# The last 256 rows of a two-layer attention and MLP kernel in two chunks of 128, and a longer planned latency for the DMAs that spread reciprocals

## The chip, the core and the metric

The kernel runs on one core of a Trainium2 chip. TensorE (PE) does the matrix products, ScalarE (ACT) the exponentials, VectorE (DVE) most other arithmetic, GpSimd (POOL) a few small sums and one kind of DMA; most DMAs are issued by SyncE (SP). The metric is the device time of one execution, in microseconds (us). Three executions of the kernel before took 1590.61, 1589.63 and 1586.18 us; their median is 1589.63 us. The trace is of one further execution, which took 1588.44 us.

## What is computed

Two equal layers are applied to x (2048 rows of 512, bf16). Each layer is attention with 32 heads of 16, and then a two-matrix MLP with 1792 hidden columns, each with a layer norm ahead of it and a residual sum behind it:

```
x = x + A(layernorm(x));  x = x + B(layernorm(x));  x = x + A(layernorm(x));  x = x + B(layernorm(x))
A(x): q, k, v = heads of x @ wqkv;  softmax(q k^T / 4) v, heads joined, @ wo
B(x): relu(x @ w1) @ w2
```

The 2048 x 2048 scores of 64 head-layers have to go through an exponential: 268 million of them. Output and inputs are bf16.

## The kernel before, in words

**Rows in chunks.** The rows are tiled by 128. A *chunk* (`chunks`, L460 to L464) is the set of query rows that goes through attention and MLP together: 512 rows (4 tiles) for all of layer one and for the first two chunks of layer two, and 256 rows (2 tiles) for layer two's last four, numbered 2 to 5; `LAST` is 5. For each chunk and each pair of heads (`T` from 0 to 3, and an even and an odd half `e`) there is a *segment* (L831): eight segments a chunk, each over 16 blocks of 128 keys and 4 row groups.

**The stream of exponentials.** The main loop (L1267) goes by slots. In each, PE makes scores into one of two groups of three PSUM banks (L1396), in units of 512 columns. In a chunk narrower than 512, a unit is several key blocks beside each other: two of 256. ACT turns three units (1536 columns) or two (1024) into exponentials with one instruction (L1405). Where it takes two, DVE makes the third by integer arithmetic (`dve_block` and `chain`, L1086 and L1126): `lin` (L1090), two `step` (L1131), two `cube` products (L1142, L1146), worked in pairs of units. PE then adds the products with the values into one PSUM bank, `ps_o` (L983). PE may repeat a round of scores in a slot where it would otherwise do too little (`times`, L1387).

**The end of a segment.** DVE copies `ps_o` to `u` (L897). Of each row's 512 or 256 sums the reciprocal is needed on all 16 lanes of a head: SP moves the sums to a small tile `c` (L902), DVE takes the reciprocal (L924), SP moves it back (L925), POOL spreads it with a further DMA to `r` (L927), and DVE multiplies (`ot`, L913). For the last segment of a chunk (`quick`, L921) the spreading is done on DVE instead (a shuffle, L937). The segment before the very last, and the last, take the reciprocal of all lanes on DVE without DMAs (`direct`, L941).

**The rest of a chunk** (`rest_of_chunk`, L795) are *groups* of PE work that fill the gaps between scores: the output projection `o_group` (L695), layer norm and transposes (`ln_rows`, `ln_groups`), the first MLP product `h_group` (L722), the second `z_group` (L762). An `h_group` fills a PSUM bank of 512 columns: one block of 128 hidden columns for a 512-row chunk, two for a 256-row chunk. The blocks of w1 (128 KB each) are loaded again for every chunk, through four buffers in turn (L710): a group's own loads are issued by SP as soon as its product is done, for the group two further on (L742 to L750).

**What sets the order.** The program writes all instructions in an order that a planner inside the kernel works out. It keeps a modelled clock of PE and of DVE (`now_pe`, `now_dve`), and the constants of L75 to L96 are its durations and latencies; `mark(key, lag=...)` records when a result is expected, and a DVE task is placed when its inputs are expected. Three of these constants are latencies of DMAs: `C_LAG` (`u` to `c`, 3.6 us), `R_LAG` (from the reciprocal through both moves to `r`, 10.5 us, L934) and `U_LAG` (from the reciprocal to `u` alone, 3.0 us). They delay nothing on the chip: every engine and queue works in the order written and waits for semaphores.

**The end of the program** (L1432 to L1528). After the last segment's value products the planner first writes whatever groups are left (`run_all`, L1436; their relu goes to ACT there, L734). Then a sequence by hand does the last chunk's rest: the output projection of its rows with the last heads from `direct` (L1461 to L1468), statistics and a reciprocal root in small DVE steps (L1469 to L1473), the second product for a row tile of the chunk before, left for this place (`half_part`, L1494), transposes, and a loop over 14 blocks of hidden columns (L1501) in which the product of a block's `h`, its relu (on DVE and ACT by turns) and the `z` product of the block before follow each other.

Of the kernel before, what the change touches and what calls it, by code (L numbers as in the profile page):

```python
# [12 lines left out]
BF16 = mybir.dt.bfloat16  # L13
# [12 lines left out]
def kernel(  # L26
# [11 lines left out]
    P = 128  # L38
# [3 lines left out]
    S, D = x_flat.shape  # L42
# [4 lines left out]
    NF = DFF // P  # L47
    NTT = S // P
    NKB = S // P
    NDC = D // P  # L50
    QS = 512
    NQS = S // QS
    TPC = QS // P
    NT = 8
# [22 lines left out]
    PE_TO_DVE, DVE_TO_PE, ACT_TO_PE, PE_TO_ACT = 220.0, 180.0, 240.0, 222.0  # L77
    DVE_TO_DVE, EVAC = 112.0, 612.0
    FLOOR = 0.56
    C_LAG, R_LAG, U_LAG = 3600.0, 10500.0, 3000.0  # L80
    VLAG = 1
    X_ISSUE, X_LAG = 1400.0, 7500.0
    RSTD_LAG = 4000.0
# [53 lines left out]
    xnT = [sb([P, NDC, QS], BF16, f"xnT{j}") for j in range(NQS)]  # L137
# [106 lines left out]
    busy = [0.0]  # L244
# [43 lines left out]
    def task(cost, fn, makes=(), deps=(), place=None):  # L288
        t = {"cost": cost, "fn": fn, "makes": makes, "deps": deps}
        dve_q.insert(len(dve_q) if place is None else place, t)  # L290
        maker.update({k: t for k in makes})
# [6 lines left out]
    def put_evac(cost, fn):  # L298
        evac.append((cost, now_pe[0] + PE_TO_DVE, fn))
# [159 lines left out]

    chunks = {(l, j): (j * TPC, TPC) for l in range(2) for j in range(NQS)}  # L460
    HALF = TPC // 2
    for n in range(4):
        chunks[1, 2 + n] = (2 * TPC + n * HALF, HALF)
    LAST = 5  # L464

    def columns(l, j):

# [118 lines left out]
    def ln_groups(tag, dst, at_column, n, war):  # L586
        groups = []
        for i in range(0, n, 2):
            hold = {}

            def piece(k):
                if not k % 2:
                    hold["b"] = bank()
                half = hold["b"].bitcast(BF16)[:, k % 2 * D : (k % 2 + 1) * D]
                ln_transpose(tag, k, half)
                if not k % 2:
                    return
                pt = hold["b"].bitcast(BF16).rearrange("p (i c f) -> p c i f", i=2, c=NDC)

                def fin():  # L600
                    a = at_column + (k - 1) * P
                    nc.vector.tensor_copy(
                        out=dst[:, :, a : a + 2 * P].rearrange("p c (i f) -> p c i f", i=2), in_=pt
                    )
                    for of in (k - 1, k):
                        mark(("xnT", tag, of))

                put_evac(609, fin)

            groups.append(  # L610
                group(
                    [(1.3, lambda k=k, piece=piece: piece(k)) for k in (i, i + 1)],
                    [("xT", tag, k) for k in (i, i + 1)] + [("xnT", tag, k) for k in (i, i + 1)],
                    [("xn", tag, k) for k in (i, i + 1)] + war,
                )
            )
        return groups
# [101 lines left out]

    w1_to_load = deque()  # L720

    def h_group(l, j, ft, war):  # L722
        n = (l * NQS + j) * NF + ft
        xj, a, w = columns(l, j)

        number = QS // w
        fts = range(ft, ft + number)
        made_here = [("h", l, j, f) for f in fts]

        def fin(b):  # L730
            out = htp[ft // 2][:, ft % 2 : ft % 2 + number, a : a + w]
            sums = b.rearrange("p (f q) -> p f q", f=number)
            if ending[0]:
                nc.scalar.activation(out=out, in_=sums, func=ACTF.Relu)  # L734
            else:
                nc.vector.tensor_scalar(  # L736
                    out=out, in0=sums, scalar1=0.0, scalar2=None, op0=ALU.max
                )
            for key in made_here:
                mark(key)  # L740

        def after():  # L742
            for f in range(number):
                load_w1(n + f + NW1)
            if w1_to_load:
                home, of = w1_to_load.popleft()
                nc.sync.dma_start(
                    out=home,
                    in_=B_w1[:, of * P : (of + 1) * P].rearrange("(c p) f -> p c f", p=P),
                )  # L750

        return mm_group(
            [
                (w1buf[(n + f) % NW1][:, c, :], xnT[xj][:, c, a : a + w])
                for f in range(number) for c in range(NDC)
            ],
            fin, made_here,
            each(w // P, "xnT", ("ln2", l, j)) + war + [("w1", n + f) for f in range(number)],
            after=after, wide_by=w, sums=number,
        )  # L760

    def z_group(l, j, i):  # L762
# [18 lines left out]
    def before(l, j):  # L781

        if (l, j) == (0, 0):
            return None
        if not j:
            return 0, NQS - 1
        rows = chunks[l, j][0] % TPC
        return max(
            (l, b) for b in range(j)
            if chunks[l, b][1] == TPC or chunks[l, b][0] % TPC == rows  # L790
        )

    w1_last = []
# [1 line left out]
    def rest_of_chunk(l, j):  # L795

        if (l, j) == (1, LAST - 2):
            for ft in range(NF):
                home = (
                    w1buf[((l * NQS + LAST) * NF + ft) % NW1] if ft < NW1  # L800
                    else (kt01 + kt2)[(ft - NW1) // 2][:, ft % 2, :].rearrange(
                        "p (c f) -> p c f", c=NDC
                    )
                )
                w1_last.append(home)
                if ft >= NW1:
                    w1_to_load.append((home, ft))
        b = before(l, j)
        xj, a, w = columns(l, j)
        n = w // P  # L810
        war_h = each(chunks[b][1], "z", *b) if b else []
        work[0:0] = [o_group(l, j, i) for i in range(n)] + ln_groups(
            ("ln2", l, j), xnT[xj], a, n, []
        )
        gs = [h_group(l, j, ft, war_h) for ft in range(0, NF, QS // w)]
        gs += [z_group(l, j, i) for i in range((l, j) == (1, LAST - 1), n)]
        if l == 0:
            if not by_dma(("ln1", 1, j)):
                gs += ln_groups(("ln1", 1, j), xnT[j], 0, TPC, [])
            gs.append(k_group(1, 0, j))  # L820
            gs += [v_group(1, kb) for kb in range(j * TPC, (j + 1) * TPC)]
            gs += [k_group(1, T, j) for T in range(1, 4)]
        return gs
# [38 lines left out]
    ended = {}  # L862
# [4 lines left out]
    def finish_segment(sg, last):  # L867
# [50 lines left out]
                mark(("ot", l, j, t, i))  # L918

        ended[l, j] = ended.get((l, j), 0) + 1  # L920
        quick = ended[l, j] == NT or sg["load"] is not None and sg["busy"]  # L921

        def recip():
            nc.vector.reciprocal(out=c, in_=c)  # L924
# [35 lines left out]
        if last:  # L960
            last_steps.append(direct)
        elif sg is segs[-2]:
            task(3100, direct_all, ots + [("m", n)], war + [("u", n)])
        else:
            task(165, recip, [("r", n)], [("c", n)], place=0)
            ready = ("r", n)
            if quick:
                task(200 + 1.05 * width, spread, [("spread", n)], [ready])
                ready = ("spread", n)
            task(105 + 1.1 * width, lambda: mul(0, width), ots + [("m", n)], [ready] + war)  # L970
# [588 lines left out]
```

The softmax here doesn't subtract the row's maximum and nothing guards it: scores larger than these inputs give would overflow.

## Time and profile before

| what | us |
|---|---|
| median of three executions | 1589.63 |
| the profiled execution | 1588.44 |
| its span, first to last instruction | 1586.6 |
| ACT busy in the span | 1545.3 |
| of it exponentials (L1405) | 1536.7 |
| DVE busy | 1506.7 |
| PE busy | 1430.4 |
| POOL busy | 101.3 |
| end of the last exponential to end of the span | 29 |

The instruction lines are the kernel's line numbers. Busy times are the union of an engine's instructions; matmuls overlap in the array, so a mean of one matmul is longer than the spacing of two. "Idle before" is time in which an engine had nothing running, with the instruction that ended it behind the arrow. A granted clock (PEclk) of 1.00 is full speed of TensorE and 0.50 half.

### The profile page before, as it was taken

The numbers are of one execution on the slowest core, as the hardware profiler recorded it, in microseconds if no ns is written. First come the engines' busy times: TensorE is split into PE (matmuls) and PEld (weight loads), VectorE is DVE, ScalarE is ACT, GpSimd is POOL, SyncE is SP. The second block draws the span as 40 slices with busy tenths as digits, with TensorE's granted clock in tenths as the row PEclk, the third lists the DMA queues.
The fourth block names the chain that finished last, engine by engine and source line by source line (L and its number), as shares of the span: only waits on it lengthen the run. The fifth ranks groups of instructions, "written<-read, shape, count | busy, mean of one in ns | idle before, by whom it ended". The sixth has DMA issues, their size and how long they took to land.

```text
span 1586.6 us, 45174 instructions
## 1 busy us (share of the span) xinstructions
PE 1430.4 (90%) x19752; PEld 536.9 (34%) x19752; DVE 1506.7 (95%) x2910; ACT 1545.3 (97%) x1383; POOL 101.3 (6%) x240
## 2 busy tenths in 40 slices
PE   8888889998899989999899998888999999999898
PEld 3222223222233322322223222223334444544454
DVE  7899999999999999999899998899999999999994
ACT  7999999999999999999999999999999999999994
POOL 2000001001010010100100001001001000010100
PEclk9999999999999999999999999999999999999998
DMA  6001101111012120120101000000210111313030
GB/s 193 15 2 26 18 9 22 39 25 25 6 19 45 23 29 7 25 48 13 26 2 28 21 2 1 2 4 9 54 25 16 40 33 27 74 26 80 13 62 15
DMA packets 128885, 45.57 MB, mean 29 GB/s; under 512 B 117840, under 2 KB 125776, under 8 KB 128688
## 3 DMA queue, kind: packets, MB, share of 16 engines
q1 hardware_dynamic: 114752, 29.36, 8.6%
q0 software_dynamic: 12592, 12.02, 4.3%
q8 instruction: 154, 2.52, 0.7%
q10 hardware_dynamic: 1344, 1.31, 0.2%
q14 instruction: 43, 0.35, 0.1%
HBM read 24.38 MB, written 2.10 MB: 17 GB/s over the span
## 4 chain that ended last, share of the span: by engine, by line
ACT 81%; PE 8%; DVE 7%; issue 2%; DMA 1%; ACTq 0%; DVEq 0%
ACT e L1405 81%; PE ps_s L1396 3%; PE ps_f L446 2%; DVE lin L1090 2%; PE ps_o L983 2%; DVE step L1131 1%; PE ps_s L1458 1%; DVE cube L1146 1%; DVE cube L1142 1%; DMA wqkv<-in_A_wqkv_dram 1%; DMA r<-u 0%; DVE ht L736 0%; DVE q L676 0%; DVE ot L913 0%; DVE stats L481 0%
## 5 line engine op out<-in xcount | busy, mean ns | idle before, releaser
L1405 ACT ACTIVATE e<-ps_s 128x1536 bf16<-128x1536 f32 (+1 forms) x1366 | 1536.7, 1362 | 8.5 <-PE ps_s L1396 8.1
L1396 PE MATMUL ps_s<-q,ktp 32*128 32x512 bf16 (+1 forms) x6136 | 608.1, 341 | 112.4 <-ACT e L1405 99.2
L983 PE MATMUL ps_o<-e,vaug 128*32 128x512 bf16 (+1 forms) x4236 | 500.8, 346 | 14.1 <-DVE u L897 8.3
L1090 DVE TENSOR_SCALAR lin<-ps_s 128x512 int16<-128x512 f32 x702 | 478.3, 685 | 24.5 <-PE ps_s L1396 18.1
L1396 PEld LDWEIGHTS <-ktp 32*128 32x128 bf16 x6136 | 200.3, 92 | 563.6 <-issue 418.9
L1131 DVE TENSOR_SCALAR step<-lin 128x1024 int16<-128x1024 int16 x702 | 275.3, 419 | 1.9 <-PE ps_o L983 0.9
L983 PEld LDWEIGHTS <-vaug 128*32 128x32 bf16 x6052 | 173.8, 95 | 300.9 <-issue 282.2
L1142 DVE TENSOR_TENSOR cube<-step 128x1024 f16<-128x1024 bf16 x351 | 238.4, 683 | 1.6 <-PE ps_o L983 0.2
L1146 DVE TENSOR_TENSOR cube<-cube,lin 128x1024 bf16<-128x1024 f16 x351 | 238.0, 679 | 0.0
L446 PE MATMUL ps_f<-w,ht 128*32 128x512 bf16 x1624 | 151.6, 381 | 1.8 <-DVE x L768 0.5
L446 PE MATMUL ps_f<-xnT,w 128*32 128x512 bf16 (+1 forms) x2016 | 146.3, 345 | 5.8 <-DVE ht L736 3.6
L983 PE MATMUL ps_o<-step,vaug 128*32 128x512 bf16 (+1 forms) x884 | 151.0, 340 | 0.0
L983 PE MATMUL ps_o<-cube,vthird 128*32 128x512 bf16 (+1 forms) x836 | 148.9, 339 | 0.0
L983 PE MATMUL ps_o<-lin,vaug 128*32 128x512 bf16 (+1 forms) x884 | 125.9, 339 | 4.6 <-DVE u L897 3.2
L927 POOL DMA_DIRECT2D r<-u x59 | 43.1, 731 | 1168.6 <-DVE lin L1090 341.7
L446 PE MATMUL ps_f<-xnT,wqkv 128*32 128x512 bf16 (+1 forms) x1312 | 109.4, 365 | 6.2 <-DVE ktp L626 1.1
L446 PE MATMUL ps_f<-wo,ot 128*32 128x512 bf16 x960 | 90.3, 381 | 1.2 <-DVE x L700 1.2
L736 DVE TENSOR_SCALAR ht<-ps_f 128x512 bf16<-128x512 f32 x105 | 72.0, 685 | 2.3 <-PE ps_f L446 1.5
L446 PEld LDWEIGHTS <-w 128*32 128x32 bf16 x2016 | 57.5, 96 | 33.9 <-issue 18.7
L676 DVE TENSOR_TENSOR q<-ps_f,masks 128x1024 bf16<-128x1024 f32 (+1 forms) x51 | 53.6, 1052 | 9.1 <-PE ps_f L446 8.1
L446 PEld LDWEIGHTS <-ht 128*32 128x32 bf16 x1624 | 46.9, 96 | 25.3 <-issue 11.9
L983 PEld LDWEIGHTS <-vthird 128*32 128x32 bf16 x836 | 43.6, 95 | 33.5 <-issue 28.7
(103 smaller groups left out, 609.4 us busy)
## 6 DMA issues: line engine op xcount, KB each, us to landing
w<-in_B_w_dram SPq DMA_DIRECT2D x130, 128.0 KB
r<-u POOLq DMA_DIRECT2D x32, 256.0 KB, 7.3
r<-u POOLq DMA_DIRECT2D x27, 128.0 KB, 4.9
out_dram<-x SPq DMA_DIRECT2D x16, 128.0 KB
x<-in_A_x_dram SPq DMA_DIRECT2D x14, 128.0 KB
w<-in_B_w_dram SPq DMA_DIRECT2D x1, 1792.0 KB
ktp<-in_B_w_dram SPq DMA_DIRECT2D x10, 128.0 KB
wqkv<-in_A_wqkv_dram ACTq DMA_DIRECT2D x2, 512.0 KB
```

The source lines that it names most:

```text
L446: nc.tensor.matmul(out[cols], lhsT[:, cols], rhs, start=i % k == 0, stop=i % k == k - 1, tile_position=(0, 32 * g), skip_group_check=True,)
L676: return nc.vector.tensor_mul(out=qbuf[n % 2][:, :, 0:w], in0=b.rearrange("p (e q) -> p e q", e=1).to_broadcast((P, 2, w)), in1=qmask.rear ...
L736: nc.vector.tensor_scalar(out=out, in0=sums, scalar1=0.0, scalar2=None, op0=ALU.max)
L927: nc.gpsimd.dma_start(out=r[:, 0:width], in_=bass.AP(tensor=sums.tensor, offset=sums.offset, ap=[list(sums.ap[0]), [0, 32], [1, width]],),)
L983: nc.tensor.matmul(ps_o[32 * g : 32 * g + 32, 0 : sg["w"]], values[:, 4 * sg["T"] + g, 2 * e : 2 * e + 32], rhs, start=g not in sg["begun" ...
L1090: first = nc.vector.tensor_scalar(out=lin[which][:, half * QS : (half + 1) * QS], in0=src, scalar1=EXP_BIAS, scalar2=0.0, op0=ALU.add, op1 ...
L1131: nc.vector.tensor_scalar(out=stair, in0=line, scalar1=keep, scalar2=put, op0=ALU.bitwise_and, op1=ALU.bitwise_or,)
L1142: (609, lambda: nc.vector.tensor_mul(out=power, in0=mantissa, in1=mantissa)),
L1146: (609, lambda: nc.vector.tensor_mul(out=power.bitcast(BF16), in0=power, in1=line.bitcast(BF16))),
L1396: nc.tensor.matmul(b[:, a : a + sg["w"]], kt[32 * g : 32 * g + 32, kc : kc + P], qbuf[sg["n"] % 2][32 * g : 32 * g + 32, sg["e"], 0 : sg[" ...
L1405: ex = nc.scalar.activation(out=eb[:, 0 : place[m]], in_=b[:, 0 : place[m]], func=ACTF.Exp, scale=1.0 / (LOG2E * UNIT),)
L1458: uses(nc.tensor.matmul(out, lhsT, rhs, start=first, stop=last), b, needs=needs)
```

## The change

Layer two's rows 1792 to 2047 become two chunks of 128, numbered 5 and 6, and `LAST` is 6. A unit of scores of such a chunk is four key blocks of 128 columns. Its segments are all `quick`, so that none of them uses the POOL DMA. An `h_group` still makes two blocks of hidden columns at most (`per_group`), now 2 x 128 columns of a bank. Transposes are written for a single tile too. The sequence by hand at the end is over one tile of 128 rows, and the tile left for `half_part` is the only one of chunk 5. `R_LAG` goes from 10.5 to 13.0 us, for the whole program. The planner lays the whole program anew with these.

```
-    C_LAG, R_LAG, U_LAG = 3600.0, 10500.0, 3000.0
+    C_LAG, R_LAG, U_LAG = 3600.0, 13000.0, 3000.0
...
-    for n in range(4):
+    for n in range(3):
         chunks[1, 2 + n] = (2 * TPC + n * HALF, HALF)
-    LAST = 5
+    chunks[1, 5] = (3 * TPC + HALF, 1)
+    chunks[1, 6] = (3 * TPC + HALF + 1, 1)
+    LAST = 6
...
-                if not k % 2:
+                m = min(2, n - i)
+                if k - i < m - 1:
                     return
...
-                put_evac(609, fin)
+                put_evac(609 if m == 2 else 342, fin)
...
+    def per_group(w):
+        return min(QS // w, 2)
+
     def h_group(l, j, ft, war):
...
-        number = QS // w
+        number = per_group(w)
...
-            after=after, wide_by=w, sums=number,
+            after=after, wide_by=w, sums=number, cost=77 + 1.045 * number * w,
...
-        gs = [h_group(l, j, ft, war_h) for ft in range(0, NF, QS // w)]
+        gs = [h_group(l, j, ft, war_h) for ft in range(0, NF, per_group(w))]
...
-        quick = ended[l, j] == NT or sg["load"] is not None and sg["busy"]
+        quick = ended[l, j] == NT or sg["load"] is not None and sg["busy"] or width == P
...
-            task(3100, direct_all, ots + [("m", n)], war + [("u", n)])
+            task(1560 * width // P, direct_all, ots + [("m", n)], war + [("u", n)])
```

Line numbers of the new kernel are 2 to 8 higher than the old ones from here on; the texts below use the old ones for what stands in both, unless they say otherwise.

More of the change, by code (lines that the diff above doesn't have):

```diff
@@ L589, in ln_groups, with piece @@
             hold = {}
-            def piece(k):
+            def piece(k, i=i, hold=hold):
                 if not k % 2:
@@ L595, in piece @@
                 ln_transpose(tag, k, half)
-                if not k % 2:
+                m = min(2, n - i)
+                if k - i < m - 1:
                     return
-                pt = hold["b"].bitcast(BF16).rearrange("p (i c f) -> p c i f", i=2, c=NDC)
+                pt = hold["b"].bitcast(BF16)[:, 0 : m * D].rearrange(
+                    "p (i c f) -> p c i f", i=m, c=NDC
+                )
                 def fin():
-                    a = at_column + (k - 1) * P
+                    a = at_column + i * P
                     nc.vector.tensor_copy(
-                        out=dst[:, :, a : a + 2 * P].rearrange("p c (i f) -> p c i f", i=2), in_=pt
+                        out=dst[:, :, a : a + m * P].rearrange("p c (i f) -> p c i f", i=m), in_=pt
                     )
-                    for of in (k - 1, k):
+                    for of in range(i, k + 1):
                         mark(("xnT", tag, of))
-                put_evac(609, fin)
+                put_evac(609 if m == 2 else 342, fin)
             groups.append(
                 group(
-                    [(1.3, lambda k=k, piece=piece: piece(k)) for k in (i, i + 1)],
-                    [("xT", tag, k) for k in (i, i + 1)] + [("xnT", tag, k) for k in (i, i + 1)],
-                    [("xn", tag, k) for k in (i, i + 1)] + war,
+                    [(1.3, lambda k=k, piece=piece: piece(k)) for k in range(i, min(i + 2, n))],
+                    [(key, tag, k) for key in ("xT", "xnT") for k in range(i, min(i + 2, n))],
+                    [("xn", tag, k) for k in range(i, min(i + 2, n))] + war,
                 )
@@ L786, in before @@
             return 0, NQS - 1
-        rows = chunks[l, j][0] % TPC
+        first, rows = chunks[l, j]
         return max(
             (l, b) for b in range(j)
-            if chunks[l, b][1] == TPC or chunks[l, b][0] % TPC == rows
+            if chunks[l, b][0] % TPC <= first % TPC < chunks[l, b][0] % TPC + chunks[l, b][1]
         )
```

## The prediction

> **What bounds the kernel now.** I read the page's busy times first, then the groups of ACT by shape, then the timeline wherever ACT's groups leave a gap, then the end.
>
> ```profile
> span 1586.6 us, 45174 instructions
> ...
> L1405 ACT ACTIVATE e<-ps_s 128x1536 bf16<-128x1536 f32 (+1 forms) x1366 | 1536.7, 1362 | 8.5 <-PE ps_s L1396 8.1
> ```
>
> The exponentials fill 1536.7 of 1586.6 us and ACT stood idle before them for 8.5 us in all. So there are four ways to move the time: the number of exponentials on ACT, the few stalls of ACT, new stalls, and the two ends. By shape:
>
> ```profile
> L1405 ACT ACTIVATE e<-ps_s 128x1536 bf16<-128x1536 f32 x663 | 1005.1, 1578 | 4.8 <-PE ps_s L1396 4.4 <-PE ps_o L983 0.3
> L1405 ACT ACTIVATE e<-ps_s 128x1024 bf16<-128x1024 f32 x702 | 760.8, 1159 | 3.6 <-PE ps_s L1396 3.6
> ```
>
> Each unit of 512 that DVE does not make costs ACT 1578 - 1159 = 0.42 us (1005.1/663 - 760.8/702 = 0.43).
>
> The largest stall of ACT, in the timeline around 400 us (start, duration, instruction, idle before):
>
> ```profile
> 397.35 0.68 DVE L1090 TENSOR_SCALAR lin<-ps_s 128x512 int16<-128x512 f32 x1
> ...
> 400.58 0.75 DVE L913 SCALAR_TENSOR_TENSOR ot<-u,masks,r 128x512 bf16<-128x512 f32 x1 [2.55 <-DMA r<-u]
> ...
> 401.99 0.82 PE L1396 MATMUL ps_s<-q,ktp 32*128 32x512 bf16 x9 [1.90 <-DVE lin L1090]
> 402.43 1.94 ACT L1405 ACTIVATE e<-ps_s 128x1024 bf16<-128x1024 f32 x2 [1.71 <-PE ps_s L1396]
> ```
>
> DVE stands 2.55 us for a spreading DMA; the next `lin`, behind it, is late; PE waits for the bank that `lin` reads; ACT waits for PE. SP's own timeline says why `r` was late:
>
> ```profile
> 384.41 6.28 SPq L571 DMA_TRANSPOSE xnT<-xn  x4
> 390.86 0.56 SPq L925 DMA_DIRECT2D u<-c  x1
> ```
>
> The reciprocal ended at 386.15 us (DVE's timeline: 385.90 plus 0.25), but its move back stood behind four transposing DMAs until 390.86; POOL's DMA began at 393.25, and the chain shows it for 7.31 us. In all 14.4 us against 10.5 planned; an undisturbed one takes 2.4 + 7.3 = 9.7.
>
> The end, in the chain of work that ended last:
>
> ```profile
> 1563.95 0.59 ACT x L1468
> ...
> 1569.69 0.61 PE ps_s L1458 x4
> ...
> 1582.59 0.69 DVE x L1525
> ```
>
> The last exponential ends at 1557.64, the last value product at 1559.25; then 4.7 us to the first copied row, 5.7 us of layer norm and transposes, 12.8 us of loop and about 4 us of copies and output DMA: 29 us with no exponential.
>
> **The change part by part.** The counts are from the instruction lists of the two built programs.
>
> *Exponentials.* 1536-wide ones go from 663 to 669, 1024-wide from 702 to 696: DVE makes three pairs fewer. 6 x 0.43 = **+2.6 us**, nothing hides it. DVE: the two narrow chunks add 15 copies of 0.28, 15 shuffles of 0.29, 13 products of 0.35, 14 reciprocals of 0.17 and 8 q's of 0.42, and drop 7 copies of 0.42, 6 products of 0.46, 6 reciprocals of 0.19, 4 q's of 0.68 and a shuffle of 0.44 (128-wide durations are the 256- and 512-wide rows continued): +9 us of busy time; three pairs at 2 x 0.68 + 2 x 0.39 + 2 x 0.68 = 3.5 us go: -10.5. That cancels, so DVE costs nothing more by itself.
>
> *R_LAG.* In the new order, the product that stalled stands 32 DVE instructions behind its reciprocal instead of 23, and the move back stands behind one transposing DMA of 1.57 us instead of four. The latency falls to about 11.3 us, under 13.0. With the 1.71 us at 402.4 go the two smaller delays behind it (the granted clock is 0.50 from 403.9 to 407.3 us, after PE's idle time; ACT's next starts are 0.27 and 1.47 us late); 1.92 + 0.27 + 1.47 = 3.65. Between 0 (another product becomes late) and -3.65 I take **-3.6**: DVE waited for `r` only twice, 2.8 us in all. Later products hold `u` and `r` longer, but three buffers over segments of 13.7 us (256 wide) leave room.
>
> *The closing sequence.* By the new lists, seven h groups of chunk 5 are still to come near the end: two stand among the last scores, five behind the last value product, ahead of the last chunk's output projection on PE's queue. Each needs two blocks of w1, whose loads are issued when the group two before it is done. A pair of loads before the change:
>
> ```profile
> 1518.50:1519.00 0.50, 0.50 (x16) 0.23 (x14) 0.50 (x2) 0.50 (x1) 0.02 (x1) 1.00 0.74 170
> 1519.00:1519.50 0.50, 0.50 (x24) 0.49 (x24) 0.47 (x2) 0.50 (x1) 0.50 (x1) 1.00 0.91 207
> 1519.50:1520.00 0.50, 0.50 (x30) 0.48 (x20) 0.50 (x2) 0.50 (x2) 0.16 (x1) 1.00 0.58 128
> ```
>
> (windows of 0.5 us; the last two columns are the DMA engines' share and GB/s). SP issued that pair from 1517.37; the bytes have passed by about 1519.9: 2.5 us, 2.75 with hand-overs. Groups three and four can start at once, five and six wait for loads released by three and four, seven for five: 0.45 + 2.75 + 0.45 + 2.75 + 0.45 = 6.85 us, then nine products of 0.216 and the drain, 2.1: 9.0 us to the copied row instead of 4.7, **+4.3**. Then one tile of statistics, not two (1.29 to 0.68), aggregation (-0.1), four transposes, not eight (-0.3): **-0.9**. The loop: per block 4 x 0.107 + 2 x 0.216 = 0.87 us of PE now; 4 x 0.055 + 0.216 = 0.43 then. But a relu of 128 columns takes 0.28 us, and from a block's last h product to its z product 0.61 pass (0.22 matmul, 0.1, 0.28), covered by only 0.43 of other products; in turn the two give (0.61 + 0.43)/2 = 0.52 a block. 12.8 becomes 8.0: **-4.8**. One copy and one output DMA: **-0.3**. Sum -1.7. PE has little to do during the load waits, and in the end now shown its clock fell after a slack stretch:
>
> ```profile
> 1550.00:1554.20 4.20, 2.79 (x59) 1.57 (x59) 4.02 (x8) 4.20 (x5) 0.00 (x0) 1.00 0.02 4
> 1554.20:1561.00 6.80, 6.80 (x65) 3.46 (x60) 3.16 (x8) 3.23 (x3) 0.00 (x0) 0.50 0.00 0
> ```
>
> (the column of 1.00 and 0.50 is the granted clock). If the nine products and a few groups fall into a half-clock stretch, they take 2.4 us more; I count 1.0 and have **-0.7** for the end. Bounds: -7 if the loads hardly count, +3 if rounds take 3.5 us at half clock.
>
> *The narrow stage.* Two chunks of 128 hold as many units (256) as one of 256, some 110 us. PE gets about 815 packs of three or four concurrent 128-column products. Nothing in the trace shows such a pack. The nearest rows from both sides: eight 128-column transposes took 0.62 us including 0.22 for the last, so 0.057 each, which is half of the 0.11 that four concurrent 256-column products take; if a pack kept 0.11, 815 x 0.054 = 44 us more. PE's slack: it waited for ACT 21.2 us between 1140 and 1555, 5.6 per 110 us; its idle time of 7 to 12 us in 110 holds that. I take 0.057, since the transposes have the same 128 columns and a fresh weight load each: nothing. [...]
>
> Then the queue: every narrow segment has two more SP moves with a planned 3.0 us for the second; from SP's issue to POOL's start behind it, 2.4 us pass now (390.86 to 393.25). At four places of the new list the move back stands directly behind three w1 loads of 0.41 us issue time each: 1.2 us against 0.6 us of room. If DVE then waits 0.6 each time, what is queued behind it are `lin`s, and ACT waits, as at 400 us. Between 0 and 4 x 0.6 = 2.4, and 0.3 for the doubled waits for `ps_o`: **+1.5**.
>
> Sum: +2.6 - 3.6 - 0.7 + 1.5 = -0.2. On the profiled execution's 1588.44 that is **1588 us**; it lay 1.2 us under the median of the three runs, inside their spread, so this is no change. About 0.3% is what a measurement of this kernel can tell from no change: 1584.9 to 1594.4.
>
> **The rivals.** *Faster, the re-laid program loses its other stalls too (0.22).* ACT also stood for about 1.0 us at 1304, 1.3 around 965 and 0.4 each at 62, 597 and 981 us: 3.5 in all, from chance meetings of queues, which another order may or may not repeat. If they go, and a round of loads takes 2.0 instead of 2.75: -0.2 - 3.5 - 1.5 - 1.5 (no queue cost) = -6.7, 1582. For it: only one long wait of ACT lies between 1140 and 1555. Against: new meetings are as likely.
>
> *Slower, PE becomes the bound of the narrow stage (0.20).* From packs above about 0.07 us on (815 x 0.013 = 11 us, the whole idle time), each further 0.01 costs 8 us; at 0.083, halfway between the rows, 815 x 0.026 - 11 = +10, so 1598; at 0.11, +33. For it: twice as many instructions for the same columns. Against: the transposes.
>
> *The longer lag does not do it (0.08):* the product is late all the same, as 14.4 is over 13.0: 1592.
>
> **How the numbers follow.** Forecast 0.50, with its own range 1583 to 1593. Faster than 0.3%: 0.06 of the forecast and 0.20 of the first rival, 0.26. Slower: 0.03 of the forecast, 0.16 of the second, 0.01 of the third, 0.20. The rest, 0.54, is no change. The range reaches to 1581 and 1598: the first rival and half of the second lie in it.
>
> **What would show it.** Right: 669 and 696 exponentials with some 2.6 us more in all; no wait of `ot` for `r` near 400 us; in the narrow stage ACT idle below 3 us and four-packs under 0.06 us; behind the last value product PE waits twice for w1 for 2 to 3 us; 27 to 30 us from the last exponential to the end. Wrong: PE busy without idle time while ACT waits for scores in the last 110 us; h groups that do not wait for w1; a new wait of DVE for a DMA over 1 us.

## The result, and the profile after

| | us | ratio to before, 95% interval |
|---|---|---|
| before, four executions | 1588.74 | |
| changed, four executions | 1590.2 (1587.6 to 1591.0) | 1.0007 (0.9988 to 1.0026) |
| changed, twelve more in a later series (before: 1589.63) | 1592.6 (1589.7 to 1596.9) | 1.0012 (1.0000 to 1.0024) |

No change that can be told, as forecast. Its parts are not small, though: each is some 0.2 to 0.6%, and they cancel. The profiled execution took 1590.3 us against 1588.44.

The page of the changed kernel, and its ACT groups by shape (count, then busy time and mean ns, then idle time before):

```profile
span 1588.3 us, 48382 instructions
...
L1413 ACT ACTIVATE e<-ps_s 128x1024 bf16<-128x1024 f32 (+1 forms) x1366 | 1539.8, 1358 | 7.1 <-PE ps_s L1404 6.6
```

```profile
L1413 ACT ACTIVATE e<-ps_s 128x1536 bf16<-128x1536 f32 x669 | 1009.1, 1572 | 6.0 <-PE ps_s L1404 5.6 <-PE ps_o L991 0.3
L1413 ACT ACTIVATE e<-ps_s 128x1024 bf16<-128x1024 f32 x696 | 750.9, 1153 | 1.1 <-PE ps_s L1404 0.9
```

The exponentials are 3.1 us longer in all, ACT's idle time before them is nearly the same (7.1 against 8.5). The program has 3208 more instructions, nearly all of them TensorE's: 21,311 products instead of 19,752. That column of the page, which the prediction read only as "twice as many instructions for the same columns", returns below.

SyncE's timeline of the changed kernel at the place of the old stall (start, duration, instruction):

```profile
385.57 1.24 SPq L573 DMA_TRANSPOSE xnT<-xn  x1
388.38 0.55 SPq L933 DMA_DIRECT2D u<-c  x1
389.05 5.91 SPq L573 DMA_TRANSPOSE xnT<-xn  x3
```

The move back (`u<-c`) now stands behind one transposing DMA, and the other three come after it. `ot` at 403.46 us waits for nothing. But two drops of the granted clock in this execution, at 383.6 and 574.7 us, are followed by 0.93 and 0.77 us of idle time of ACT.

The end of the changed kernel, in the chain of work that ended last:

```profile
1560.47 4.11 DMA w<-in_B_w_dram
...
1564.63 0.65 PE ps_s L446 x16
1565.29 2.44 DMA w<-in_B_w_dram
...
1567.78 1.04 PE ps_f L446 x32
1568.82 3.36 PE ps_s L1466 x9
...
1572.20 0.59 ACT x L1476
```

The chain goes twice through a load of w1; in TensorE's own timeline four of the five closing groups wait for w1, by 0.66, 2.69, 0.40 and 0.66 us. The nine products of the projection then take 3.36 us, not 2.1, as the clock is 0.50 from 1564.6 to 1571.4 us. From the last exponential to the end pass 28.75 us (before 28.96).

### The profile page after: what moved, and what is told of

Its sections match the earlier page's. It is cut to its first block, busy times and chain, and to the rows that moved or that the text cites. A ratio compares the mean times of both kernels' runs of the same rounds, so it can differ in the third digit from the quotient of the medians.

```text
span 1588.3 us, 48382 instructions
## 1 busy us (share of the span) xinstructions
PE 1434.6 (90%) x21311; PEld 552.5 (35%) x21311; DVE 1503.0 (95%) x2947; ACT 1549.2 (98%) x1387; POOL 96.8 (6%) x243
## 4 chain that ended last, share of the span: by engine, by line
ACT 78%; PE 10%; DVE 8%; issue 2%; DMA 2%; SPq 1%; ACTq 0%; DVEq 0%
ACT e L1413 78%; PE ps_s L1404 3%; PE ps_o L991 3%; PE ps_f L446 3%; DVE lin L1098 2%; DVE step L1139 1%; DVE cube L1154 1%; DVE cube L1150 1%; DMA w<-in_B_w_dram 1%; PE ps_s L1466 1%; DMA wqkv<-in_A_wqkv_dram 1%; DVE ht L744 0%; SPq L719 0%; DVE q L681 0%; DVE ot L921 0%
## 5 line engine op out<-in xcount | busy, mean ns | idle before, releaser
L1413 ACT ACTIVATE e<-ps_s 128x1024 bf16<-128x1024 f32 (+1 forms) x1366 | 1539.8, 1358 | 7.1 <-PE ps_s L1404 6.6
L1404 PE MATMUL ps_s<-q,ktp 32*128 32x512 bf16 (+2 forms) x6699 | 608.3, 325 | 112.1 <-ACT e L1413 102.1
L991 PE MATMUL ps_o<-e,vaug 128*32 128x512 bf16 (+2 forms) x4682 | 496.7, 328 | 8.9 <-DVE u L905 2.7
L991 PE MATMUL ps_o<-step,vaug 128*32 128x512 bf16 (+2 forms) x950 | 159.5, 327 | 0.0
L446 PE MATMUL ps_f<-xnT,w 128*32 128x512 bf16 (+2 forms) x2144 | 150.1, 339 | 6.1 <-DVE ht L744 3.1
L991 PE MATMUL ps_o<-cube,vthird 128*32 128x512 bf16 (+2 forms) x888 | 143.5, 327 | 0.0
L991 PE MATMUL ps_o<-lin,vaug 128*32 128x512 bf16 (+2 forms) x950 | 125.6, 328 | 6.2 <-DVE u L905 3.7
L446 PE MATMUL ps_f<-xnT,wqkv 128*32 128x512 bf16 (+2 forms) x1376 | 107.8, 351 | 5.5 <-DVE ht L744 1.1
L744 DVE TENSOR_SCALAR ht<-ps_f 128x512 bf16<-128x512 f32 (+1 forms) x107 | 72.8, 681 | 3.4 <-PE ps_f L446 2.7
L681 DVE TENSOR_TENSOR q<-ps_f,masks 128x1024 bf16<-128x1024 f32 (+2 forms) x55 | 54.3, 987 | 7.9 <-PE ps_f L446 5.7
L446 PEld LDWEIGHTS <-ht 128*32 128x32 bf16 x1680 | 48.8, 96 | 28.5 <-issue 12.8
L483 DVE BATCH_NORM_STATS2 stats<-x 128x6 f32<-128x512 bf16 x64 | 43.1, 684 | 12.8 <-ACT x L1476 10.9
```

The lines of the kernel that those rows point to most:

```text
L446: nc.tensor.matmul(out[cols], lhsT[:, cols], rhs, start=i % k == 0, stop=i % k == k - 1, tile_position=(0, 32 * g), skip_group_check=True,)
L483: nc.vector.bn_stats(out=stats[ln_n(tag)][:, i, :], in_=x_t[tt][:])
L681: return nc.vector.tensor_mul(out=qbuf[n % 2][:, :, 0:w], in0=b.rearrange("p (e q) -> p e q", e=1).to_broadcast((P, 2, w)), in1=qmask.rear ...
L744: nc.vector.tensor_scalar(out=out, in0=sums, scalar1=0.0, scalar2=None, op0=ALU.max)
L991: nc.tensor.matmul(ps_o[32 * g : 32 * g + 32, 0 : sg["w"]], values[:, 4 * sg["T"] + g, 2 * e : 2 * e + 32], rhs, start=g not in sg["begun" ...
L1404: nc.tensor.matmul(b[:, a : a + sg["w"]], kt[32 * g : 32 * g + 32, kc : kc + P], qbuf[sg["n"] % 2][32 * g : 32 * g + 32, sg["e"], 0 : sg[" ...
```

## The experiments

Medians of several runs scatter here by the clock. Each run lists its mean granted clock, and within every kernel of the table below the times lie on a line against it, 0.74 to 1.05 us longer for each 0.001 of clock lost (before: 0.91, 29 runs, residuals of 0.42). So beside the measured ratio a second number stands below: where that line meets a clock of 1.000. It is an extrapolation of 3 to 8 us, with a standard error of 0.2 to 0.9 us (1.4 for e2, which has six runs), and only explains; the ratio is what was measured. For the kernel before it is 1583.9 in the series of e1 to e4, 1583.4 in that of e5 to e8, 1584.3 in that of e10 and e11, and 1584.5 in that of e12.

| run | exponentials 1536 / 1024 | ratio to before, 95% interval | at clock 1.000 |
|---|---|---|---|
| e1, longer lag alone | 663 / 702 | 0.9982 (0.9967 to 0.9998) | 1580.6 |
| e2, chunks alone | 673 / 692 | 1.0059 (1.0041 to 1.0077) | 1592.2 |
| e5, changed kernel | 669 / 696 | 1.0012 (1.0000 to 1.0024) | 1586.8 |
| e7, the kernel before once more (lag 10.5) | 663 / 702 | 1.0003 (0.9991 to 1.0016) | 1584.0 |
| e10, before, move back on POOL | 663 / 702 | 1.0001 (0.9986 to 1.0016) | 1583.1 |
| e11, chunks alone, move back on POOL | 673 / 692 | 1.0031 (1.0012 to 1.0049) | 1586.3 |
| e3, changed, w1 kept | 669 / 696 | 0.9987 (0.9974 to 0.9999) | 1581.9 |
| e4, changed, end kept busy | 669 / 696 | 0.9998 (0.9985 to 1.0011) | 1586.6 |
| e8, as e3 with lag 12.5 | 667 / 698 | 1.0014 (0.9997 to 1.0030) | 1586.6 |
| e6, four chunks of 128 | 673 / 692 | 1.0025 (1.0011 to 1.0039) | 1589.6 |
| e12, as e6, fewer instructions | 673 / 692 | 1.0023 (1.0007 to 1.0039) | 1589.3 |

### The two parts alone

e1 is the kernel before with `R_LAG` 13000.0.

> The kernel before with R_LAG at 13.0 us and nothing else. Exponentials stay at 663 and 702. If the longer lag removes the stall at 400 us and the program is otherwise undisturbed, the span falls by 3.6 us, to about 1583, and DVE no longer waits for a spreading DMA. If stalls of a re-laid program are as many as before wherever they stand (what the changed kernel's trace suggests, with a new drop of the granted clock at 384 and 575 us), the time is that of before within 2 us.

e2 is the changed kernel with `R_LAG` 10500.0.

> The changed kernel with R_LAG back at 10.5 us. Its exponentials are 673 and 692, four more units of 512 on ACT than the changed kernel, ten more than before. By the account that counts units, 4 x 0.43 = 1.7 us more than the changed kernel, plus up to 3.6 for the stall near 400 us if it comes back: 1592 to 1596. By the rival that R_LAG matters only by chance meetings, the same as the changed kernel within 2 us.

The lag alone is faster by 0.18%, 2.9 us; the chunks alone are slower by 0.59%, 9.4 us, which is more than either account of e2 had (1592 to 1596; measured 1599.7). The lag is thus worth 2.9 us in the old program and some 8 us (1.0059 against 1.0007 or 1.0012) in the new. Part of that is the low clock of e2's six runs (0.9905 in the mean, against 0.9936 for before in the same series): at clock 1.000, each against the kernel before of its series, the lag is worth 3.3 us in the old program and 5.0 in the new, which the errors don't tell apart. The counts do: in the new program the lag also takes four exponentials from 1536 to 1024 columns (673 to 669), in the old none. In the trace of e2 the old wait is back, and gone in e1 and in the changed kernel. VectorE's timeline of e2:

```profile
406.15 0.75 DVE L921 SCALAR_TENSOR_TENSOR ot<-u,masks,r 128x512 bf16<-128x512 f32 x1 [2.33 <-DMA r<-u]
```

e5 is the changed kernel once more.

> The changed kernel as it is, for a direct comparison with the others of this batch and with the copy that keeps w1. Theory (no change in the sum: exponentials +2.6, the r wait -3.6, end -0.7 to 0, narrow stage +1.5 to 2.8): median 1588 to 1591 us, ratio to before 0.998 to 1.001. Rival (the four runs so far met an unlucky clock): 1585 or less, ratio under 0.997.

It fell a little above the range given, 1592.6 us; its ratio, 1.0012, is just outside too. The rival (an unlucky clock in the first four) is out.

### What the longer lag does

Does the longer lag help because it puts `ot` further behind the reciprocal, or because the new order changes what stands ahead of the move back on SyncE's queue? e7 was to be the kernel before with `R_LAG` 15500.0.

> The kernel before with R_LAG at 15.5 us instead of 10.5 and nothing else; 663 and 702 exponentials as before. Theory (what the longer lag does is to put the multiplication behind the arrival of r): no wait of VectorE for r above 0.6 us, the same gain as with 13.0, 2 to 4 us, median 1585 to 1587, ratio 0.997 to 0.999. Rival (the gain with 13.0 was the luck of one new order): ratio 0.9995 or above, with the wait gone and stalls of TensorScalar or scores at other places in its stead.

The kernel that ran under this label has `R_LAG` at 10500.0; it is the kernel before, line for line. So it tests neither theory nor rival, and no run here has a lag of 15.5 us. What it gives is how far apart two series of one program come out (1.0003, and 0.6 us at clock 1.000), and a second trace of the kernel before. In it `ot` waits again; SyncE's timeline of e7, then VectorE's:

```profile
388.27 5.54 SPq L571 DMA_TRANSPOSE xnT<-xn  x4
393.98 0.55 SPq L925 DMA_DIRECT2D u<-c  x1
```

```profile
403.72 0.75 DVE L913 SCALAR_TENSOR_TENSOR ot<-u,masks,r 128x512 bf16<-128x512 f32 x1 [1.81 <-DMA r<-u]
```

The traces have the two halves of the question apart. The third column is the time from the end of the reciprocal to the landing of `r`, the fourth how far behind the end of the reciprocal `ot` had its turn (its start less its wait), in us:

| trace | transposing DMAs ahead of the move back | `r` landed after | turn of `ot` after | wait of `ot` |
|---|---|---|---|---|
| before | 4 | 14.4 | 11.9 | 2.55 |
| e7, before once more | 4 | 13.7 | 11.9 | 1.81 |
| e2, chunks alone | 4 | 14.2 | 11.9 | 2.33 |
| e8, lag 12.5 (below) | 2 | 13.1 | 13.05 | 0.08 |
| e1, longer lag alone | 1 | 10.9 | 15.4 | 0 |
| changed kernel | 1 | 10.7 | 15.1 | 0 |

The longer lag did two things at once. It put `ot` 3 us later, and it had the program laid in an order in which three of the four transposes stand behind the move back. By these rows either would have been enough: 10.7 and 10.9 are under 11.9, and 15.1 and 15.4 are over 14.4. e8 speaks for the later place by itself, as `r` took 13.1 us there, more than 11.9, and `ot` hardly waits; no run holds the queue as it was and moves `ot` alone.

e10 takes the move off that queue and leaves all else:

```
-            nc.sync.dma_start(out=sums, in_=c)
+            (nc.sync if quick else nc.gpsimd).dma_start(out=sums, in_=c)
```

> The kernel before (R_LAG 10.5 us, 663 and 702 exponentials in the same order) with one edit: the move back of the reciprocals to u is issued on GpSimd's queue, ahead of the spreading DMA that follows it there, and no longer on SyncE's, where four transposing DMAs stood ahead of it. Theory (the wait of VectorE for r at 400 us came from SyncE's queue; the longer lag helped only where the new order happened to put the move ahead of three of the four transposes): the wait at 400 us is gone without any longer lag, the stalls of ScalarE at 399 to 405 us (3.6 us) too, 2.5 to 4 us less than before, 1586 to 1587, ratio 0.997 to 0.9985. Rival (the latency of the spreading DMA itself, 7.3 to 8.4 us, is the long part, and two DMAs behind each other on GpSimd make it longer): a wait of 1 us or more stays, also at other segments, and the time is that of before or above.

POOL's timeline of e10 (the idle time before in brackets), and VectorE's:

```profile
390.36 0.77 POOL L925 DMA_DIRECT2D u<-c  x1 [3.45 <-DVE c L924]
394.30 0.69 POOL L927 DMA_DIRECT2D r<-u  x1 [3.17 <-DMA u<-c]
```

```profile
401.88 0.74 DVE L913 SCALAR_TENSOR_TENSOR ot<-u,masks,r 128x512 bf16<-128x512 f32 x1
```

The four transposes still run on SyncE (388.33 us, 6.13). `r` now lands 11.6 us behind the reciprocal, `ot` keeps its turn at 11.8 and no longer waits, with the lag at 10.5. So the queue is shown as the cause of the long latency and with it of the wait. ACT's idle time from 395 to 410 us goes too (3.2 us in the trace before, none here), and so does the drop of the granted clock: in all three traces with the wait (before, e7, e2) a drop to 0.50 begins 3.3 to 3.9 us behind the start of `ot` (before: 400.58 and 403.89), and in e1, e8, e10, e11 and the changed kernel none lies within 10 us behind it. The gain in time that the theory expected is not shown: 1.0001. Its runs had a mean clock of 0.9926, those of before in the same series 0.9945; at clock 1.000 it is 1.2 us ahead of before in the same series, where the first of the old stalls alone took 1.9. Why its clock fell more often stays open.

e11 is the same edit in the chunks alone.

> The chunks of 128 alone (R_LAG back at 10.5 us, 673 and 692 exponentials, as in e2_chunks_only) with the move back on GpSimd's queue as in e10_before_move_on_pool. Theory (the r wait of 2.3 us at 406 us in e2_chunks_only was SyncE's queue too): that wait and its stalls gone, 3 to 4 us under e2_chunks_only's ratio of 1.0059, so 1.003 to 1.004, 1594 to 1596; the rest above the changed kernel is four more 1536-column exponentials (1.7 us) and the other meetings of that order. Rival (without the longer lag other multiplications wait, so that the lag is needed for itself): 1.005 to 1.007, with waits of VectorE for r elsewhere.

1.0031 against 1.0059 for e2: 4.4 us by the ratios, with the intervals overlapping a little (from 1.0041, to 1.0049), in the range expected. In its trace `r` lands 11.6 us behind the reciprocal, `ot` has its turn at 11.8 and doesn't wait there; two others wait 0.3 us or less. So taking the move off this queue gives about half of the 8 us that the longer lag gives with the chunks; within the errors it may be nearly all of it.

### The closing groups

e3 keeps the loaded w1 blocks for the last two chunks instead of one, so that the closing groups wait for no load:

```
-        if (l, j) == (1, LAST - 2):
+        if (l, j) == (1, LAST - 3):
...
+    def w1_of(l, j, ft, n):
+        return w1_last[ft] if (l, j) == (1, LAST - 1) else w1buf[n % NW1]
...
-                (w1buf[(n + f) % NW1][:, c, :], xnT[xj][:, c, a : a + w])
+                (w1_of(l, j, ft + f, n + f)[:, c, :], xnT[xj][:, c, a : a + w])
```

> The changed kernel, but the second-to-last chunk's h groups read w1's blocks from the places where they are kept for the last chunk; these are loaded one chunk earlier, so the five closing groups wait for no load. Same exponentials, same five groups after the last value product. If the loads pace the end, from last value product to the first copied row 12.0 us become about 5 (five groups at 0.5 and nine products at 0.22), the clock does not drop there, and the time falls by 6 to 8 us, to 1583. If the end is bounded by something else on PE or ACT, or the granted clock alone makes it long, less than 3 us.

From the last exponential to the end pass 22.5 us instead of 28.75, and no clock drop falls into the closing. From the last value product to the copied row: 5.9 us instead of 12.0. The chain of e3:

```profile
1568.54 0.78 PE ps_s L446 x56
1569.44 0.45 PE ps_f L446 x27
1569.88 1.38 issue
...
1573.58 0.59 ACT x L1484
```

The loads are shown as the price of the closing. The total is 0.9987 against 1.0007 and 1.0012 of the changed kernel, 3 to 4 us less where 6 to 8 were expected. What remains in it is a wait of 1.38 us of TensorE for nothing that the profile knows ("issue"), of the kind that the last experiments measure.

e4 leaves the loads and has TensorE multiply something useless (12, 3 and 3 products of 512 columns into a free bank) while it waits:

> The changed kernel with 18 products of 512 columns added behind the closing groups (12, 3 and 3; into a bank that nobody reads), where PE waits for w1. They add work and should fit into the waits at full clock. If half of the closing excess comes from the clock that PE's idle time loses, the nine products ahead of the copied row take 2.1 instead of 3.4 us, the groups 0.45 instead of 0.8, and the time falls by 2 to 2.5 us. If the loads alone pace it, no change, or up to 1 us more.

The clock stays at 1.00 to the end, the nine products take 2.06 us instead of 3.36, and the end is 26.84 us instead of 28.75. Half clock thus cost some 1.9 us there. The total (0.9998) doesn't resolve it.

e8 is e3 with `R_LAG` 12500.0, whose order has one pair of 1536-column exponentials fewer.

> The changed kernel with the w1 blocks kept for the last two chunks, as in the run e3_w1_kept, and R_LAG at 12.5 us, with which the order comes out at 667 and 698 exponentials (0.9 us less). Theory (terms add): 0.9 us under e3_w1_kept, 1586 to 1588, ratio 0.997 to 0.9995 against before, 2 to 4 us faster than the changed kernel of this batch; the end from the last exponential 22 to 24 us. It would then not beat the kernel before with the longer lag alone (0.9982). Rival (each new order brings or loses stalls of 2 to 4 us at will): anywhere from 1583 to 1592.

The rival was right: 1.0014, 4 us above e3 instead of 0.9 below, though its end is nearly as short (23.1 us) and no `ot` waits over 0.1 us. New meetings took the difference, as far as the two traces tell: in e8's ACT stands idle around 470, 780, 985, 1179 and 1315 us for some 3.5 us more than in e3's. Two of TensorE's waits behind that, in e8's timeline:

```profile
469.32 0.38 PE L539 MATMUL ps_f<-ident,xn 128*128 128x128 bf16 x4 [0.92 <-DVE ktp L631]
...
1178.30 0.62 PE L999 MATMUL ps_o<-e,vaug 128*32 128x512 bf16 x8 [1.15 <-DVE u L911]
```

So a new order moved this kernel by some 4 us here.

### The narrow stage

In the changed kernel ACT waits five times for scores between 1450 and 1560 us, 0.22 to 0.82 us each. The loss is a little more, because exponentials usually overlap: their mean durations are 1.57 us for 1536 columns and 1.15 for 1024, their usual spacing (the median from one start to the next) 1.33 and 0.90. Counted as lateness, the spacing beyond this usual one, the five are 0.41 to 0.94 us, 2.8 in all. The longest wait, in the timeline:

```profile
1523.96 0.23 PE L991 MATMUL ps_o<-e,vaug 128*32 128x128 bf16 x1 [0.84 <-issue]
...
1524.68 1.45 ACT L1413 ACTIVATE e<-ps_s 128x1536 bf16<-128x1536 f32 x1 [0.82 <-PE ps_s L1404]
```

TensorE stops for 0.84 us, and the profile shows nothing that it waits for. e6 doubles the stage:

```
-    for n in range(3):
+    for n in range(2):
...
-    chunks[1, 5] = (3 * TPC + HALF, 1)
-    chunks[1, 6] = (3 * TPC + HALF + 1, 1)
-    LAST = 6
+    for n in range(4):
+        chunks[1, 4 + n] = (3 * TPC + n, 1)
+    LAST = 7
```

> Layer two's last 512 rows as four chunks of 128, so that the narrow stage doubles; R_LAG stays 13.0 us; 673 and 692 exponentials instead of 669 and 696 (+1.7 us). Theory (the narrow stage costs only the small stalls of ACT, 2.8 us per 256 rows in the trace after against about 1 in a stage of 256-column units): 1.7 + 1.8 = 3.5 us more than the changed kernel, 1592 to 1595, ratio to the kernel before 1.001 to 1.004; value products of 128 columns stay at 0.40 to 0.41 us for sixteen; ACT stalls under 7 us between 1330 and 1560 us. Rival (TensorE is near its bound in the narrow stage, and twice as long a stage uses up its slack): 10 us or more on top, 1600 and above, with ACT waiting for scores throughout those 220 us.

1594.1 us and 1.0025 are where the theory had them. But the lateness of the exponentials is 11 us between 1400 and 1560 (7.1 us of it idle time of ACT), more than the theory's 7; a shorter end (24.25 us) may have paid for that. TensorE's timeline of e6:

```profile
1527.66 0.34 PE L446 MATMUL ps_f<-xnT,w 128*32 128x128 bf16 x9 [0.91 <-issue]
1531.96 0.41 PE L1404 MATMUL ps_s<-q,ktp 32*128 32x128 bf16 x9 [0.78 <-issue]
1536.25 0.34 PE L1404 MATMUL ps_s<-q,ktp 32*128 32x128 bf16 x9 [0.83 <-issue]
```

Different lines and operations, but a period of 4.3 us. Counted through the trace's list of products and weight loads of TensorE, each of these gaps ends at number 182 of a group of 256. Nine such gaps of over 0.2 us lie behind 1429 us, 5.4 us in all, none ahead of it, and each ends 2.3 to 2.9 us after a packet of 16,384 bytes of the DMA queue named "instruction" began. The two of the changed kernel, at 1511.90 and 1523.96 us, end at number 182 too, 2.51 and 2.31 us after such a packet began. e9 measures it by itself: 64 packs of four concurrent products of 512 columns, 192 of 256 columns and 384 of 128, which wait for nothing.

```
+    for w, packs in ((512, 64), (256, 192), (128, 384)):
+        for _ in range(packs):
+            for g in range(4):
+                nc.tensor.matmul(
+                    ps_s[1 - slot[0] % 2][32 * g : 32 * g + 32, 1, 0:w],
+                    ident[:, 32 * g : 32 * g + 32], wo[:, 0, 0:w], start=True, stop=True,
+                    tile_position=(0, 32 * g), skip_group_check=True,
+                )
```

> The changed kernel with three rows of extra products behind the five closing groups, none of which waits for anything: 64 packs of four concurrent products of 512 columns, 192 packs of 256, 384 packs of 128, each product with its weight load (their sums are not used; the time is longer by these 75 us or so). It measures the spacing of packs by itself. Theory (in the narrow stage TensorE runs out of instructions: the gaps without a releaser stand at one place of every 256 of its recorded instructions, 2.3 to 2.9 us after a packet of its instruction queue began): packs of 512 at 0.216 us and of 256 at 0.11 us with no gap; packs of 128 at 0.056 us inside a stretch of 32 packs (256 instructions, 1.8 us), then a gap of 0.4 to 1.2 us, so 0.07 to 0.09 us a pack sustained. Rival (TensorE takes such packs at 0.056 us for as long as it likes, and the gaps of the narrow stage come from something else, a wait that the profile does not show): no gaps over 0.2 us in the 384 packs, 21 to 22 us in all. Second rival (the spacing itself rises when packs are sustained): an even 0.08 us a pack without gaps.

TensorE's timeline of e9 (x is the number of products in a stretch), and the instruction queue in the window 1606 to 1650 us (packets, MB):

```profile
1568.00 37.89 PE L1449 MATMUL ps_s<-wo,ident 128*32 128x512 bf16 x1151
1606.65 1.97 PE L1449 MATMUL ps_s<-wo,ident 128*32 128x128 bf16 x128 [0.76 <-issue]
...
1618.43 1.97 PE L1449 MATMUL ps_s<-wo,ident 128*32 128x128 bf16 x128 [1.77 <-issue]
1622.45 1.97 PE L1449 MATMUL ps_s<-wo,ident 128*32 128x128 bf16 x128 [2.05 <-issue]
```

```profile
q8 instruction: 11, 0.18, 1.6%
```

At a granted clock of 1.00 packs of 512 columns follow each other in 0.216 us, and packs of 256 in 0.109, without a gap. Packs of 128 go at 0.056 us there, but in stretches of 128 products and 128 loads: eleven times TensorE stands idle ahead of the next, 0.76 to 2.05 us with nothing that the profile shows it waiting for. A stretch and its gap are 3.7 to 4.0 us, 0.119 us a pack in the mean. Eleven packets in 44 us are 4.0 us each, nearly the same period. So in this row TensorE takes 256 instructions in about 4 us, 64 to 68 a us, and one packet came for each 256. The packs of 256 took 73 a us for 20.9 us and had no gap. At the rate of the row behind them, 1340 to 1420 of their 1536 instructions would have come in that time and some 110 to 200 before it (an estimate from these rates; no run shows it). Both rivals are out, and the gaps are larger than the theory had them (up to 2.05 us, expected 0.4 to 1.2).

Between 1450 and 1510 us the kernel before takes 36 instructions of TensorE per us (2185 products and weight loads in the window), the changed one 59 (3550) and e6 64 (3863). e12 is e6 with fewer: a group's product in the narrow stage and the closing is one matmul over 128 weight columns instead of four concurrent ones over 32, with the same streamed columns:

```
+                    if narrow[0]:
+                        nc.tensor.matmul(
+                            out, lhsT[:, 0:P], rhs, start=i % k == 0, stop=i % k == k - 1,
+                            skip_group_check=True,
+                        )
+                        continue
                     for g in range(4):
```

> The kernel of e6_four_narrow (four chunks of 128; every instruction of ScalarE, VectorE and SyncE in the same order) with one edit: in the narrow stage and the closing, a group's product is one matmul over all 128 weight columns instead of four concurrent ones over 32 each, with the same streamed columns; 1260 products and 1260 weight loads fewer of 22,823 each. Theory (the gaps of TensorE without a releaser in the narrow stage are its instruction queue, which e9_packs_alone showed to give 256 instructions per 3.5 to 4.0 us): with some 50 instructions of TensorE per us instead of 64 between 1360 and 1575 us, the gaps of 0.7 to 0.9 us at one place of every 256 instructions go (5.4 us in e6_four_narrow's trace), and ScalarE's stalls of 1400 to 1560 us fall from 11 to 5 to 7 us; 4 to 6 us less than e6_four_narrow, ratio 0.999 to 1.000. Rival (the gaps come from something else, or the full-width products cost as much as they save because they wait for the array): the stalls stay within 2 us of 11, ratio 1.0015 to 1.004.

The rate falls to 52 per us (3134 from 1450 to 1510), and the gaps are gone. TensorE's waits of e6 from 1360 to 1565 us that end with "issue" (total, times, longest):

```profile
PE ps_f L446 <- issue: 2.7, 5, 0.9
PE ps_s L1404 <- issue: 1.6, 2, 0.8
PE ps_o L991 <- issue: 1.1, 2, 0.7
```

In e12 the same list has none. ACT's waits from 1400 to 1560 us, of e6 and of e12:

```profile
ACT e L1413 <- PE ps_s L1404: 6.9, 13, 1.0
```

```profile
ACT e L1422 <- PE ps_s L1413: 2.0, 7, 0.4
```

ACT's idle time there falls from 7.1 to 2.9 us, and the lateness of its exponentials from 11 to about 8 us, less than expected (5 to 7). The time stays (1.0023 against 1.0025, where 0.999 to 1.000 was expected). So it is shown that the gaps go with the rate of TensorE's instructions (nine at 64 a us, none at 52), and not that their removal makes this kernel faster: the two intervals leave a difference of up to 3 us either way open. The profile of e6 is of its slowest run, 1602.17 us of a median of 1594.1; but every drop of its clock lies ahead of 1106 us or behind 1579, outside this stage. In e12 the lateness ahead of that is larger (3.0 instead of 1.8 us from 1300 to 1400), where TensorE's gaps were few.

## Why the prediction was right, and where it was wrong

**The sum** was -0.2 us, and the chip gave +1.5 (four runs) and +1.9 (twelve), inside the range and inside "no change". By the medians of the twelve it is +3.0 and at an equal clock +3.4 (1586.8 against 1583.4 in one series), so it was too low by 2 to 4 us. The parts as measured below (+3.1, -2.9, -0.2, +2.4) give +2.4. That the sum came this close is in part luck, as errors of opposite sign in the end cancelled, and the term of the narrow stage stood for a wait that didn't come.

**Exponentials, +2.6:** 669 and 696 as counted; the busy time grew by 3.1.

**R_LAG, -3.6:** the wait went, the lag alone measured -2.9, and the reason held: "The latency falls to about 11.3 us, under 13.0" is 10.7 in the trace, behind one transposing DMA, and `ot` has its turn 15.1 us behind the reciprocal instead of 11.9. Either alone would have been enough by these numbers. e10 shows the queue's part without the lag; the lag's part without the queue was not run. That e10 gains nothing that can be told in the total leaves open how much of the 2.9 us is this wait.

**The end, -0.7:** -0.2, from two errors of opposite sign. The term "+4.3" for the groups behind the w1 loads was +7.3: the first round took 4.11 us, not 2.75 (SyncE's queue has a third load there, of a kept block, which may be why), and half clock cost some 1.9, not 1.0. Against that, 1.0 us less passed between the last exponential and the last value product, which the sum didn't have. The layer norm (4.84 against 5.7) and the loop (7.7 against 12.8, so -5.1 for the -4.8) came as worked out.

**The narrow stage, +1.5:** about +2.4 (the five late exponentials, 2.8 us, against 0.4 in the same stretch before). The step that failed is "Then the queue": no wait of VectorE for a move behind w1 loads was found. What TensorE waited for there, besides ACT, was the copy to `u` after a segment (six times, 2.1 us); twice, for 0.35 and 0.84 us, it stood with no releaser in the profile, at number 182 of 256 as in e6, and the prediction had no term for that.

**The rivals.** "PE becomes the bound" was refuted as priced (the packs take 0.056 us, and 0.40 to 0.41 us for sixteen value products) but had a truth that it didn't name: with nothing between them, packs of 128 columns come at 0.119 us in the mean (e9), in stretches with the period of the instruction queue's packets. At 59 instructions a us the changed kernel has two gaps of 0.35 and 0.84 us, at 64 the doubled stage has nine. "The re-laid program loses its other stalls too" held for the old ones (those at 1304 and 965 us are gone from the trace after) and failed as new ones came. That the longer lag "does not do it" didn't come: `ot` waits for nothing in the traces of e1 and of the changed kernel.

**A version that beats the kernel before**, if by little, is that kernel with the longer lag alone, 0.9982 (0.9967 to 0.9998). e3 with 0.9987 (0.9974 to 0.9999) is as good within its interval.

## What to carry to other kernels

When a longer planned latency makes a wait go, read two things in the traces before and after: how far behind its source the waiting instruction has its turn, and what stands ahead of the transfer in its queue. A new plan may have changed both. The chunks of 128 took TensorE from 36 products and weight loads a us to 59, and to 64 in the doubled stage; count them in the stage, and compare with what a row of products that wait for nothing takes (64 to 68 a us in e9, with two short gaps in the changed kernel at 59). In a kernel whose parts cancel, measure each alone: here -0.2% and +0.6% stood behind "no change".

## What the runs showed of the hardware

- In e9's row of 128-column packs TensorE took 256 instructions in 3.7 to 4.0 us, and the queue named "instruction" moved 11 packets, 0.18 MB, in 44 us. The idle time between the stretches has no releaser in the profile and stands at one fixed number of each 256 (181 or 182 in the list of records, in the changed kernel, e3, e6 and e9 alike).
- Four transposing DMAs took 6.28 us of SyncE's queue in before, 5.54 in e7 and 6.13 in e10, and the move behind them began 4.7 us (before) and 4.0 us (e7) after its reciprocal was done.
- The granted clock fell to 0.50 for 3.41 or 6.83 us at a time in the traces of before and of the changed kernel. Before's drops, at 403.9, 963.7 and 1554.2 us, lie 164 and 173 times 3.413 us apart, and the changed kernel's, at 383.6, 574.7 and 1564.6 us, 56 and 290 times. Within a kernel a run is 0.74 to 1.05 us longer for each 0.001 of mean clock lost; in the 29 runs of before beside e1 to e4 that line leaves 0.4 us of a scatter of 2.4 (standard deviations). Which stretch drops is not settled.
